# Turning an intermediate by DMA transposes instead of on TensorE, and moving its producer to another PSUM pool

## Chip, cores, metric

One core of a Trainium2 chip. The metric is the device time of one execution in microseconds (us); lower is better. The core's engines are called PE (TensorE matmul), PEld (its weight loads), DVE (VectorE), ACT (ScalarE), POOL (GpSimd) and SP (SyncE, which here only issues DMAs). L394 is line 394 of the kernel that the profile belongs to; the changed file has shifted lines (M4 is L414 before and L418 after, M5 L443 and L447, M2 L376 and L377, scores L253 and L254).

## The reference, cut to what matters

```
attention: 8 batches, 8 heads, 576 positions, head size 64, window of 32 plus 8 global positions
x  = attention output as [batch, 576, 512]
h  = relu(xT @ w_tok1) @ w_tok2            # over the tokens:  M1 (relu), M2
u  = x + hT
out = u + relu(u @ w_ch1) @ w_ch2          # over the channels: M4 (relu), M5
```

M4 multiplies over the channels of u, which M2 leaves with the tokens on the partitions. So u has to be turned first: M3.

## The kernel before

The batches are pipelined. While M5 of batch b runs, M2 and M3 of batch b+1 and the score steps S and GK of batch b+2 are woven between its units; this stage ("the M5 stage of b") is where the change works. PSUM has three pools: `psS` (two buffers of two banks), `psV` (one buffer of two banks) and `psM` (two buffers of one bank, for M4 and M5). PSUM is the memory into which PE writes its results; a buffer goes to the next user only when the engine that reads it (DVE or ACT here) is done. "Exps" are the exponentials of the scores on ACT, "masks" the multiplications of these by the window mask on DVE (four in a row, 2.45 us together), GK the scores against the global positions, and a "unit" of M5 three matmuls. "Start to start" is the time from the start of one group of PE instructions to the start of the next.

```python
def M2(b, part, get):                       # part 0: tokens 0-255, 1: 256-511, 2: the last 64
    ps = get([P, 2, 512])
    ...                                     # 4, 4 or 2 matmuls
    if part < 2: nc.vector.tensor_add(out=s["u16"][...], in0=x16[...], in1=ps)
    else:        nc.vector.tensor_add(out=s["ul"][r], in0=x16[r, NT - 1], in1=ps[r, 0])

def M3(b, part, get):
    if part < 2:
        pu = get([P, 2, 4, P], F16)
        for i in range(2):
            for cc in range(4):
                nc.tensor.transpose(out=pu[:, i, cc, :], in_=s["u16"][:, 2*part + i, P*cc : P*cc + P], identity=ident)
        nc.vector.tensor_copy(out=s["uT"][...], in_=pu)
    else: ...                               # the remainder: odd batches only, for two batches at once

def M4(b, j): ...                           # 4 matmuls, rhs = all 512 tokens of uT; relu on ACT
def S_step(b, hg, part):                    # takes BOTH buffers of psS
    tiles = [pss([P, 2, 512]) for i in range(2)]
    S_mm(...); then exps on ACT             # after parts 1, two units later: four masks on DVE

def phase_m(b):
    u = [(0.9, M2 part 0 in psv), (0.9, M2 part 1 in pss), (0.5, M2 part 2 in pss)]
    u += [(0.5, M3 part 0 in psv), (0.5, M3 part 1 in pss)] + [(0.3, M3 part 2 in psv)]   # the last: odd b

def phase_s(b): return [(0.5, S step) x 4] + [(0.9, GK in psv)]
def mix(m, s): return m[:2] + s[:1] + m[2:3] + s[1:2] + m[3:4] + s[2:3] + m[4:] + s[3:]
# merge(sparse, dense) spreads such a list over the units of M5 (3 matmuls each) by the weights
```

The softmax here doesn't subtract the row's maximum and nothing guards it: scores larger than these inputs give would overflow.

## Time and profile before

| | before |
|---|---|
| device time, median of the three runs known before the prediction | 338.13 us (337.34 to 340.27) |
| profiled span | 336.1 us |
| PE busy | 316.1 us, 94% |
| length of the M5 stages of batches 2 to 6 | 18.85, 20.31, 18.43, 20.31, 13.63 us |

A stage runs from the start of its first M5 matmul to the start of the next M4. Odd stages have 20 units of M5 and even ones 16; the last has no scores beside it. The profile lines behind this table are in the prediction.

### The profile page before, as it was taken

The numbers are of one execution on the slowest core, as the hardware profiler recorded it, in microseconds if no ns is written. First come the engines' busy times: TensorE is split into PE (matmuls) and PEld (weight loads), VectorE is DVE, ScalarE is ACT, GpSimd is POOL, SyncE is SP. The second block draws the span as 40 slices with busy tenths as digits, with TensorE's granted clock in tenths as the row PEclk, the third lists the DMA queues.
The fourth block names the chain that finished last, engine by engine and source line by source line (L and its number), as shares of the span: only waits on it lengthen the run. The fifth ranks groups of instructions, "written<-read, shape, count | busy, mean of one in ns | idle before, by whom it ended". The sixth has DMA issues, their size and how long they took to land.

```text
span 336.1 us, 7493 instructions
## 1 busy us (share of the span) xinstructions
PE 316.1 (94%) x3092; PEld 162.2 (48%) x3092; DVE 193.9 (58%) x361; ACT 158.1 (47%) x295; POOL 75.5 (22%) x154
## 2 busy tenths in 40 slices
PE   7499999988999999999999999999999999999994
PEld 2236443634465445444565446444565446444641
DVE  7698686758566487356762486457573475162021
ACT  5482584125862663528443654438442554403600
POOL 5794160181341032101410033002400000000000
PEclk9789999999999999999999999999999999999999
DMA  7999979999999979503980158001000111011013
GB/s 158 184 246 225 172 135 175 226 181 248 230 194 250 181 221 240 103 34 91 249 179 2 62 170 209 0 34 64 33 2 23 41 68 30 0 64 62 2 62 94
DMA packets 55702, 41.55 MB, mean 124 GB/s; under 512 B 40948, under 2 KB 46964, under 8 KB 55668
## 3 DMA queue, kind: packets, MB, share of 16 engines
q1 hardware_dynamic: 50100, 36.59, 45.4%
q0 software_dynamic: 5568, 4.49, 8.7%
q8 instruction: 24, 0.39, 0.5%
q14 instruction: 10, 0.08, 0.1%
HBM read 36.12 MB, written 9.44 MB: 136 GB/s over the span
## 4 chain that ended last, share of the span: by engine, by line
PE 78%; ACT 7%; DVE 6%; DMA 5%; issue 2%; POOL 1%; SPq 0%; ACTq 0%; DVEq 0%; POOLq 0%
PE op L443 23%; PE b1p L414 22%; PE s L253 5%; PE hp L376 5%; PE a1p L360 4%; DMA q<-in_q_dram 4%; PE b1lp L430 3%; DVE e_all L279 3%; ACT e_all L262 3%; PE w L102 3%; PE pv L335 3%; PE pv L327 2%; PE pv L340 2%; PE gk L294 2%; PE pu L394 2%
## 5 line engine op out<-in xcount | busy, mean ns | idle before, releaser
L414 PE MATMUL b1p<-uT,wc 128*128 128x512 f16 x384 | 92.9, 379 | 1.9 <-DVE b L418 0.8
L443 PE MATMUL op<-wc,b 128*128 128x512 f16 x384 | 94.6, 379 | 0.0
L420 ACT ACTIVATE b<-b1p 128x512 f16<-128x512 f32 x90 | 53.9, 599 | 62.6 <-PE b1p L414 62.3
L443 PEld LDWEIGHTS <-b 128*128 128x128 f16 x384 | 34.8, 97 | 38.8 <-issue 4.2
L414 PEld LDWEIGHTS <-wc 128*128 128x128 f16 x384 | 34.2, 97 | 39.7 <-issue 5.3
L279 DVE TENSOR_TENSOR e_all<-e_all,bandm 128x1000 f16<-128x1000 f16 x64 | 42.0, 717 | 19.1 <-ACT e_all L268 19.0
L262 ACT ACTIVATE e_all<-s 128x800 f16<-128x800 f32 x32 | 25.1, 838 | 38.9 <-PE s L253 38.6
L447 DVE TENSOR_TENSOR osb<-u,op 128x512 f32<-128x512 f16 x32 | 21.9, 686 | 31.5 <-PE op L443 29.4
L381 DVE TENSOR_TENSOR u<-x,hp 128x1024 f16<-128x1024 f16 x14 | 17.1, 1222 | 38.9 <-PE hp L376 38.9
L282 POOL COPY eg<-e_all 128x160 f16<-128x160 f16 x14 | 4.6, 329 | 143.1 <-DVE e_all L279 143.1
L253 PE MATMUL s<-qT,kT 32*128 32x200 f16 (+1 forms) x640 | 22.0, 245 | 7.6 <-DVE qT L202 4.9
L347 DVE TENSOR_TENSOR x<-pv,rr 128x512 f16<-128x512 f32 (+1 forms) x40 | 27.6, 691 | 1.5
L335 PE MATMUL pv<-vsh,e_all 128*128 128x66 f16 x320 | 27.6, 193 | 0.0
L144 POOL CAST k<-k 128x576 f16<-128x576 f32 x28 | 18.7, 698 | 39.5 <-DMA k<-in_k_dram 22.0
L197 POOL CAST vsh<-v 128x512 f16<-128x512 f32 x38 | 24.0, 667 | 11.6 <-DMA v<-in_v_dram 11.6
L335 PEld LDWEIGHTS <-e_all 128*128 128x128 f16 x320 | 24.0, 98 | 4.8
L140 ACT CAST q<-q 128x576 f16<-128x576 f32 x28 | 18.6, 682 | 14.1 <-DMA q<-in_q_dram 7.5
L253 PEld LDWEIGHTS <-kT 32*128 32x128 f16 x640 | 12.6, 95 | 23.4 <-issue 19.3
L340 PE MATMUL pv<-vsh,e_all 128*128 128x66 f16 x256 | 23.4, 193 | 0.0
L102 PE MATMUL w<-zz 128*128 128x512 f16 x66 | 21.9, 448 | 1.3 <-DVE p_i L153 1.3
L376 PE MATMUL hp<-a,w 128*128 128x512 f16 x72 | 19.3, 378 | 2.7 <-ACT a L363 1.6
L327 PE MATMUL pv<-rf,lf 128*128 128x264 f16 x80 | 21.7, 275 | 0.0
(134 smaller groups left out, 354.5 us busy)
## 6 DMA issues: line engine op xcount, KB each, us to landing
q<-in_q_dram SPq DMA_DIRECT2D x64, 128.0 KB
out_dram<-osb SPq DMA_DIRECT2D x32, 256.0 KB
k<-in_k_dram SPq DMA_DIRECT2D x14, 576.0 KB
v<-in_v_dram SPq DMA_DIRECT2D x24, 256.0 KB
v<-in_v_dram SPq DMA_DIRECT2D x16, 192.0 KB
wc<-in_moe_w_ch_dram POOLq DMA_DIRECT2D x6, 512.0 KB, 10.0
q<-in_q_dram SPq DMA_DIRECT2D x16, 64.0 KB
out_dram<-osb SPq DMA_DIRECT2D x8, 128.0 KB
```

Source lines behind the costliest of these rows:

```text
L102: nc.tensor.matmul(ps, lhsT=zz[:, 0:P], rhs=zz, start=True, stop=True)
L253: nc.tensor.matmul(tiles[r // 2][:, r % 2, off : off + n], lhsT=kT[rs, P * c : P * c + P, e], rhs=qf[rs, lo : lo + n, e], start=(e == 0), ...
L262: nc.scalar.activation(out=e2[:, :, 1:3, 64:EW], in_=ps[:, :, 0:400].rearrange("p h (c x) -> p h c x", c=2), func=AF.Exp, scale=scale)
L279: nc.vector.tensor_mul(out=eh, in0=eh, in1=bandm)
L327: nc.tensor.matmul(ps[:, hf, 0 : 4 * VW], lhsT=lfs[b % 2][:, QS * tau - sh : QS * tau - sh + P], rhs=s["rf"][:, 4 * hf : 4 * hf + 4, :], s ...
L335: nc.tensor.matmul(o, lhsT=e_all[:, h, tau, QS - sh : QS - sh + P], rhs=vs[:, tau, h, :], start=False, stop=last and tau == NT - 1,)
L340: nc.tensor.matmul(o, lhsT=e_all[:, h, tau + 1, 0:P], rhs=vs[:, tau + 1, h, :], start=False, stop=last)
L347: nc.vector.tensor_tensor(out=x16[r, tau, :].rearrange("p (f h x) -> p f h x", f=2, h=4), in0=pq[r, :, :, 0:D], in1=rr[r].unsqueeze(3).to_ ...
L376: nc.tensor.matmul(ps[:, i, :], lhsT=w2[:, ch, P * tau - sh : P * tau - sh + P], rhs=s["a1"][:, ch, :], start=(ch == 0), stop=(ch == 1),)
L414: nc.tensor.matmul(ps, lhsT=wc1[:, cc, P * j : P * j + P], rhs=s["uT"][:, cc, :], start=(cc == 0), stop=(cc == 3))
L420: nc.scalar.activation(out=s["b1"][:, j, :], in_=ps, func=AF.Relu)
L443: nc.tensor.matmul(ps, lhsT=w, rhs=wc2[:, j, :], start=(j == 0), stop=(j == NJ - 1))
```

## The change

It takes M3 off PE for batches 3 to 7: u goes from SBUF to SBUF through DMA transposes issued on SyncE. With M3 out of PSUM, all three parts of M2 of these batches draw on `psv`, which leaves `psS` to the scores. And the list for the stage becomes M2, S, M2, S, M2, S, S, GK, with the scores' weights raised from 0.5 to 1.6, which spreads them over the M5 units. The layout of uT changes to make each transpose's output contiguous.

```diff
+TDMA = 3
 def M3(b, part, get):
-            s["uT"] = mb.tile([P, 4, 512], F16, ...)
+            s["uT"] = mb.tile([P, 4, 4, P], F16, ...)
+        if b >= TDMA:
+            if part < 2:
+                nc.sync.dma_start_transpose(out=s["uT"][:, 2*part : 2*part + 2], in_=s["u16"][:, 2*part : 2*part + 2])
+            else:
+                nc.sync.dma_start_transpose(out=s["uTl"], in_=s["ul"])
 def M4(b, j):
-  rhs=s["uT"][:, cc, :]
+  rhs=s["uT"][:, :, cc, :]
 def phase_m(b):
+        if b >= TDMA:
+            u = [(c, lambda i=i: M2(b, i, psv)) for i, (c, _) in enumerate(u)]
+            return [(c, lambda f=f, i=i: (f(), M3(b, i, None)) if i < 2 or b % 2 else f()) for i, (c, f) in enumerate(u)]
 def mix(m, s):
+        if len(m) == 3:
+            s = [(1.6, f) for _, f in s[:4]] + s[4:]
+            return m[:1] + s[:1] + m[1:2] + s[1:2] + m[2:] + s[2:]
```

(Cut: the copies into the new layout for batches 0 to 2.)

More of the change, by code (lines that the diff above doesn't have):

```diff
@@ L388, in M3 @@
         if part == 0:
-            s["uT"] = mb.tile([P, 4, 512], F16, tag="uT", name=f"uT_{b}")
-        if part < 2:
+            s["uT"] = mb.tile([P, 4, 4, P], F16, tag="uT", name=f"uT_{b}")
+        if b >= TDMA:
+            if part < 2:
+                nc.sync.dma_start_transpose(out=s["uT"][:, 2 * part : 2 * part + 2], in_=s["u16"][:, 2 * part : 2 * part + 2])
+            else:
+                s["uTl"] = mb.tile([P, 4, P], F16, tag="uTl", bufs=1, name=f"uTl_{b}")
+                nc.sync.dma_start_transpose(out=s["uTl"], in_=s["ul"])
+        elif part < 2:
             pu = get([P, 2, 4, P], F16, name=f"pu_{b}_{part}")
@@ L396, in M3 @@
                     )
-            nc.vector.tensor_copy(
-                out=s["uT"][:, :, 256 * part : 256 * part + 256].rearrange("p c (i x) -> p c i x", i=2),
-                in_=pu.rearrange("p i c x -> p c i x"),
-            )
+            nc.vector.tensor_copy(out=s["uT"][:, 2 * part : 2 * part + 2], in_=pu)
         else:
@@ L414, in M4 @@
             nc.tensor.matmul(
-                ps, lhsT=wc1[:, cc, P * j : P * j + P], rhs=s["uT"][:, cc, :], start=(cc == 0), stop=(cc == 3)
+                ps, lhsT=wc1[:, cc, P * j : P * j + P], rhs=s["uT"][:, :, cc, :], start=(cc == 0), stop=(cc == 3)
             )
@@ L555, in M3t @@
         if tau == 0:
-            s["uT"] = mb.tile([P, 4, 512], F16, tag="uT", name=f"uT_{b}")
+            s["uT"] = mb.tile([P, 4, 4, P], F16, tag="uT", name=f"uT_{b}")
         pu = get([P, 4, P], F16, name=f"pu0_{b}_{tau}")
@@ L559, in M3t @@
             nc.tensor.transpose(out=pu[:, cc, :], in_=s["u16"][:, tau, P * cc : P * cc + P], identity=ident)
-        nc.scalar.copy(out=s["uT"][:, :, P * tau : P * tau + P], in_=pu)
+        nc.scalar.copy(out=s["uT"][:, tau], in_=pu)
     def X_units(b):
```

## The prediction

> **What bounds the kernel now.** I read the page first, then the stages by windows, then TensorE (PE) in order of time, then the other engines in the same stretch. M1 and M2 are the token products of a batch, M3 turns its u, M4 and M5 are its channel products, S and GK the scores of a later batch, PV the attention output.
>
> ```profile
> PE 316.1 (94%) x3092; PEld 162.2 (48%) x3092; DVE 193.9 (58%) x361; ACT 158.1 (47%) x295; POOL 75.5 (22%) x154
> ...
> PEclk9789999999999999999999999999999999999999
> DMA  7999979999999979503980158001000111011013
> ...
> PE 78%; ACT 7%; DVE 6%; DMA 5%; issue 2%; POOL 1%; SPq 0%; ACTq 0%; DVEq 0%; POOLq 0%
> ```
>
> PE is busy 94% of the span, no other engine above 58%, and the chain that ended last is 78% PE. The DMA row: full up to slice 16 (134 us), nearly empty from slice 25 (210 us) on. So PE time removed from the later batches counts in full, and transfers there find a free path.
>
> The M3 work sits in the stage in which M5 of batch b runs beside M2 and M3 of batch b+1 and the scores of b+2. The windows over this stage for b = 2 to 6 (columns: stretch, length, busy us and count of each engine, granted clock, DMA share, GB/s):
>
> ```profile
> 141.80:160.65 18.85, 18.01 (x191) 8.41 (x190) 11.04 (x17) 10.53 (x22) 1.55 (x3) 1.00 0.24 76
> 180.05:200.36 20.31, 20.08 (x201) 9.30 (x199) 11.92 (x17) 10.62 (x22) 1.56 (x4) 1.00 0.28 90
> 216.94:235.37 18.43, 18.01 (x191) 8.40 (x190) 11.03 (x17) 10.63 (x22) 2.16 (x4) 1.00 0.12 45
> 254.78:275.09 20.31, 20.08 (x202) 9.30 (x200) 11.91 (x17) 8.39 (x18) 0.32 (x1) 1.00 0.15 53
> 291.67:305.30 13.63, 13.63 (x80) 6.79 (x78) 7.01 (x9) 0.60 (x1) 0.00 (x0) 1.00 0.16 59
> ```
>
> The clock is full, DVE and ACT have room, DMA is at 0.12 to 0.28. Inside the third of these, PE in order of time:
>
> ```profile
> 222.55 0.82 PE L443 MATMUL op<-wc,b 128*128 128x512 f16 x3
> 223.53 0.59 PE L376 MATMUL hp<-a,w 128*128 128x512 f16 x2 [0.16 <-ACT e_all L262]
> ...
> 226.54 0.61 PE L394 MATMUL pu<-ident,u 128*128 128x128 f16 x8
> 226.99 0.81 PE L443 MATMUL op<-wc,b 128*128 128x512 f16 x3
> 227.73 0.90 PE L253 MATMUL s<-qT,kT 32*128 32x200 f16 x16
> 228.56 0.82 PE L443 MATMUL op<-wc,b 128*128 128x512 f16 x3
> 229.54 0.61 PE L394 MATMUL pu<-ident,u 128*128 128x128 f16 x8 [0.16 <-ACT e_all L262]
> 229.98 0.81 PE L443 MATMUL op<-wc,b 128*128 128x512 f16 x3
> ```
>
> Two readings. Eight transposes (L394) hold PE from 226.54 to 226.99: 0.45 us, or 56 ns each; the duration of one in its row, 219 ns, overlaps its neighbours and is not the cost. And three M5 matmuls take 0.65 us (229.98 to the next start at 230.63), but after 222.55 the M2 starts only at 223.53: 0.33 us lost, released by the exp of the scores (ACT, L262). Scores take both buffers of their PSUM pool; M2 parts 1 and 2 and M3 part 1 draw from that same pool, so they wait for the exps. That is the wait which the second half of the change attacks.
>
> **What the Trainium skill says.** "Perfetto Trace Analysis", section "Optimization Strategy": the same gap repeating on the saturated engine can mean that PSUM is short for the next tile. The trace agrees: the gap before M2 part 2 returns in all four stages with scores (0.3 to 0.4 us). "VectorE: DVE Perf Modes", section "The three transpose paths": a 128x128 bf16 transpose takes 390 ns on TensorE and 1309 ns by the DMA crossbar. For PE the trace decides, 56 ns of PE time in a stream; it has no DMA transpose. "DMA: Bandwidth & Descriptors": section "Anatomy of one DMA — SWDGE (gpsimd) path" gives a fixed cost of about 2.0 us, and "Latency and other measured facts" an effective 261 GB/s for DMA transposes. On the fixed cost this trace only shows a store on the other kind of queue:
>
> ```profile
> 331.56 0.69 DVE L450 TENSOR_TENSOR osb<-ul,op 128x512 f32<-128x512 f16 x1 [1.90 <-PE op L443]
> 332.28 1.11 SPq L452 DMA_DIRECT2D out_dram<-osb  x2
> ```
>
> SyncE needs 0.55 us to issue each of the two last stores, and the span ends at 336.07, 2.7 us after the second issue: the same order as 2.0.
>
> **The change, part by part.** (1) Removed from PE: batches 3 to 7 lose 16 transposes each, and 3, 5 and 7 the 4 of the shared remainder: 92 in all, 92 x 56 ns = 5.1 us, all in a stage that PE fills. This counts in full. (2) Removed from DVE: 10 copies of 0.69 us and 3 of 0.41 us, 8.1 us. DVE is busy some 11 of 18 to 20 us there, so this is worth nothing directly. (3) PSUM: M2 now draws on the PV pool, which is idle in this stage but for GK at its end. I added up the PE waits tied to the score pool from start-to-start times. Stage b=2: 0.33 before M2 part 2, 0.28 to 0.35 inside the third score step, 0.75 before M3 part 1, 1.4 together. b=4: 0.33 + 0.28 + 0.33 = 0.94. b=3 and 5: 0.39 each. b=6 has no scores and no loss. Sum 3.1 us. The new order spaces the score steps 2 to 4 us apart, and the exps of one need 1.7 us (two of 0.84) or 2.2 us (measured from the end of a part-1 step at 225.9 to the release inside the next at 228.1), so most of it goes. I take 2.6. Single-buffered, M2 part 1 must wait until the add has read part 0; the add ends 1.4 us after part 0 (0.20 us start delay + 1.22 us of L381), and 2.6 us of M5 lie between: no wait. The 0.34 us lost at the start of M4 after the even stages, where an M5 add stands behind the masks on DVE, stays.
>
> (4) Added: per batch two DMA transposes of 256 KB (eight 128x128 blocks each), and one of 128 KB for odd batches, on SyncE. My estimate for one of 256 KB: issue 0.6 to 1.5 us, 256 KB at the skill's 261 GB/s 1.0 us, fixed 2.0 us: 3.6 to 4.5, call it 4.7 with a little delay at the queue. Time to hide it: I worked through the order of the units by their weights, with the durations of this trace (M5 unit 0.65, M2 0.86/0.86/0.43, scores 0.55/0.53, GK 1.19). In stages 2 to 5 M2 part 1 ends at 5.5 to 6.2 us, its add 1.4 later, and M4 of that batch starts at 16 us (even) or 18.5 (odd): 9 to 11 us, hidden. In stage 6 there are no scores to spread it: M2 part 1 comes after nine of sixteen M5 units, ends at 7.55, the add at 8.97, and M4 of batch 7 is due at 12.52. 3.55 us are there for 4.7, so PE stalls some 1.2 us, once. The 128 KB transfer of the remainder is needed only after all of M4 (10 us) and is hidden. (5) The layout of uT changes M4's moving operand to four runs of 128 elements; I expect no change of its 216 ns.
>
> Sum: 338.1 - 5.1 - 2.6 + 1.2 = **331.6 us**, 1.9% less.
>
> **Rivals.** *The transfer becomes the bound.* If the eight blocks of a transfer go one after another at the skill's 1309 ns, one takes 10.5 us and the two of a batch 21. In stage 6 the first starts at 4.2 us, the second ends at 25, M4 stalls 12.7 us; stages 2 to 5 stall some 7 us each; total near 370. Against it: the same page calls this path one with about 90% of the DMA bandwidth, and the order of the units looks placed for a latency of several us. A middle form, 6 to 8 us per transfer, stalls only batch 7, by 2.5 to 4.5 us: 333 to 335. *The gain moves to another wait.* Without the pool wait PE may catch up with the exps, the q casts between them on ACT (0.7 us each), or the M5 adds behind the masks on DVE; then only the transposes are won: 338.1 - 5.1 + 1.2 = 334. For it: at b=2 two casts stood before the exps and cost 0.75 us; against: ACT is at 10.6 of 18 to 20 us. *SyncE in order.* A transpose that waits for u holds the stores and loads behind it. SyncE mostly waits for M5 adds anyway, the loads for batch b+4 stand after the transposes, and three output buffers cover 7.8 us: I expect nothing. *Everything hidden*, with a transfer under 3.5 us and all 3.1 us of waits gone: 338.1 - 8.2 = 329.9.
>
> **Range and chances.** The first sum and the hidden case span 329.9 to 331.6, the lost-gain and middle cases 333 to 335, and the serial case lies far above. I put 8 in 10 on 329.0 to 338.0. The line of 2% is at 331.4, next to my number, so faster by over 2% has 0.46, within 2% 0.44, slower 0.10, which is the serial transfer.
>
> **What would show it.** Right: no L394 or L404 work in stages 2 to 6; these stages shorter by 1.1 to 2.5 us with scores and by 1.1 without; the lines with a wait on L262 gone from M2; M4 of batch 7 starting 1 to 2 us after the last M5 of batch 6, released by the DMA of uT. Wrong: a DMA wait of uT before M4 of batches 3 to 6 (transfer over 9 us), a stall of over 5 us before batch 7, M4 matmuls above 216 ns apart, or the lost time back as waits of the score steps on ACT.

## The result, and the profile after

| | before | after |
|---|---|---|
| median | 337.85 us | 328.60 us (328.19 to 329.14) |
| ratio of the fast runs | | 0.9715 (0.9673 to 0.9757) |
| profiled span | 336.1 us | 327.4 us |

A ratio is the mean time of one kernel's fast runs over that of the other's fast runs of the same rounds, so not quite the ratio of the medians. In a later group of runs the unaltered changed kernel gave 329.04 us against 337.57, ratio 0.9757 (0.9742 to 0.9773). By the two ratios the change is faster by 2.4 to 2.9%; 328.6 lies 0.4 us below the predicted range.

The page after, the lines that answer to those of before:

```profile
PE 308.2 (94%) x3000; PEld 156.3 (48%) x3000; DVE 186.5 (57%) x348; ACT 158.0 (48%) x295; POOL 75.3 (23%) x154
...
DMA  7999969999999969914891559025101320043012
```

92 matmul records are gone, 8 us of PE's busy time (in which durations count, not the time that PE was held), and the DMA row shows new work after slice 20. The windows of the same five stages (columns as in the prediction):

```profile
141.82:158.06 16.24, 16.24 (x171) 7.13 (x170) 9.45 (x14) 10.53 (x22) 0.94 (x2) 1.00 0.42 104
177.46:196.30 18.84, 18.84 (x186) 8.32 (x184) 10.59 (x15) 10.64 (x22) 0.94 (x2) 1.00 0.46 123
212.88:229.12 16.24, 16.24 (x172) 7.14 (x171) 9.45 (x14) 10.53 (x22) 1.55 (x3) 1.00 0.42 90
248.52:267.35 18.83, 18.83 (x185) 8.32 (x182) 10.59 (x15) 8.38 (x18) 0.32 (x1) 1.00 0.30 84
283.93:296.45 12.52, 12.52 (x60) 5.66 (x59) 5.11 (x6) 0.60 (x1) 0.00 (x0) 1.00 0.39 105
```

PE is now busy for the whole of every stage (16.24 of 16.24 us, before 18.01 of 18.85). The stages are shorter by 2.61, 1.47, 2.19, 1.48 and 1.11 us, 8.86 in all, and the span by 8.7: the result lies in these five stages. Of the other stages from M4 of batch 1 on none differs by over 0.02 us but the last, from the first M5 of batch 7 to the end of the last store: 17.87 us against 17.66. Of the 8.86, the removed transposes are 92 x 56 ns = 5.15; the last stage shows it pure, 20 x 56 ns = 1.12 against 1.11 measured. The other 3.71 us are waits that went. PE in order of time in the third of these stages:

```profile
217.55 1.03 PE L377 MATMUL hp<-a,w 128*128 128x512 f16 x4
218.41 1.46 PE L447 MATMUL op<-wc,b 128*128 128x512 f16 x6
219.80 0.60 PE L254 MATMUL s<-qT,kT 32*128 32x136 f16 x24
220.34 1.47 PE L447 MATMUL op<-wc,b 128*128 128x512 f16 x6
221.65 0.59 PE L377 MATMUL hp<-a,w 128*128 128x512 f16 x2
```

The M2 part 2 (the group of two on L377) follows the M5 units with no "idle before" mark; before, it had one, released by the exps. And the start of M4 of batch 7, all engines in order of time:

```profile
291.68 1.22 DVE L382 TENSOR_TENSOR u<-x,hp 128x1024 f16<-128x1024 f16 x1 [0.82 <-PE hp L377]
292.93 1.25 SPq L393 DMA_TRANSPOSE uT<-u  x1
...
296.45 1.03 PE L418 MATMUL b1p<-uT,wc 128*128 128x512 f16 x4
```

The add of M2 part 1 ends at 292.90, the transpose is issued at once, and M4 starts at 296.45, exactly when it is due (stage length 12.52, as worked out): the predicted stall is not there. The same 3.5 us in windows of half a microsecond:

```profile
293.50:294.00 0.50, 0.50 (x4) 0.22 (x3) 0.37 (x1) 0.00 (x0) 0.00 (x0) 1.00 0.00 0
294.00:294.50 0.50, 0.50 (x4) 0.19 (x2) 0.32 (x1) 0.00 (x0) 0.00 (x0) 1.00 0.75 151
295.50:296.00 0.50, 0.50 (x4) 0.19 (x2) 0.50 (x1) 0.00 (x0) 0.00 (x0) 1.00 1.02 381
```

The last two columns are the DMA share and GB/s. Nothing moves in the 1.25 us that SyncE needs to issue; then the DMA engines fill up. By the trace's DMA records the 1024 packets of 256 bytes start between 294.1 and 295.6 (a store of M5 output starts before they end).

### The profile page after: what moved, and what is told of

Same layout as the page of the kernel before. It is cut to its first block, busy times and chain, and to the rows that moved or that the text cites. A ratio compares the mean times of both kernels' runs of the same rounds, so it can differ in the third digit from the quotient of the medians.

```text
span 327.4 us, 7329 instructions
## 1 busy us (share of the span) xinstructions
PE 308.2 (94%) x3000; PEld 156.3 (48%) x3000; DVE 186.5 (57%) x348; ACT 158.0 (48%) x295; POOL 75.3 (23%) x154
## 4 chain that ended last, share of the span: by engine, by line
PE 71%; DMA 14%; DVE 4%; SPq 4%; ACT 3%; POOL 2%; issue 1%; POOLq 0%; DVEq 0%; ACTq 0%
PE op L447 26%; PE b1p L418 21%; DMA q<-in_q_dram 7%; PE hp L377 5%; DMA v<-in_v_dram 4%; PE a1p L361 4%; PE s L254 4%; PE b1lp L434 3%; SPq L95 2%; DMA wc<-in_moe_w_ch_dram 2%; PE pv L336 2%; DVE e_all L280 2%; PE pv L328 2%; PE pv L341 2%; PE gk L295 1%
## 5 line engine op out<-in xcount | busy, mean ns | idle before, releaser
L447 PE MATMUL op<-wc,b 128*128 128x512 f16 x384 | 92.5, 379 | 0.0
L263 ACT ACTIVATE e_all<-s 128x800 f16<-128x800 f32 x32 | 25.2, 841 | 29.1 <-PE s L254 28.9
L254 PE MATMUL s<-qT,kT 32*128 32x200 f16 (+1 forms) x640 | 20.8, 244 | 6.9 <-DVE qT L203 4.4
L254 PEld LDWEIGHTS <-kT 32*128 32x128 f16 x640 | 11.9, 95 | 22.2 <-issue 18.3
L377 PE MATMUL hp<-a,w 128*128 128x512 f16 x72 | 19.3, 379 | 1.9 <-ACT a L364 1.5
```

Source lines behind the costliest of these rows:

```text
L254: nc.tensor.matmul(tiles[r // 2][:, r % 2, off : off + n], lhsT=kT[rs, P * c : P * c + P, e], rhs=qf[rs, lo : lo + n, e], start=(e == 0), ...
L263: nc.scalar.activation(out=e2[:, :, 1:3, 64:EW], in_=ps[:, :, 0:400].rearrange("p h (c x) -> p h c x", c=2), func=AF.Exp, scale=scale)
L377: nc.tensor.matmul(ps[:, i, :], lhsT=w2[:, ch, P * tau - sh : P * tau - sh + P], rhs=s["a1"][:, ch, :], start=(ch == 0), stop=(ch == 1),)
L447: nc.tensor.matmul(ps, lhsT=w, rhs=wc2[:, j, :], start=(j == 0), stop=(j == NJ - 1))
```

## The experiments

The table gathers the stage lengths from the profiles, which are steadier than whole times: the M5 stage of batch 0, long before the stages that differ, took between 21.5 and 24.4 us from one profile to the next, of this kernel and of others. That alone moves whole times by up to 3 us, and the stages below do not show it. Most of it goes with the granted clock: the four profiles with 24.3 to 24.4 us there (`e2_dma_old_pool`, `e3_layout_only`, `e4_late13`, `e7_pe_new_order`) show a clock of 0.5 for 3.4 us from about 73 us on, the ten with 21.5 to 22.5 us do not.

| M5 stage of batch | 2 | 3 | 4 | 5 | 6 | sum |
|---|---|---|---|---|---|---|
| before | 18.85 | 20.31 | 18.43 | 20.31 | 13.63 | 91.5 |
| pools alone | 19.17 | 19.77 | 19.17 | 19.83 | 13.93 | 91.9 |
| change, M2 parts 1 and 2 in the score pool | 18.52 | 20.01 | 18.52 | 20.07 | 12.52 | 89.6 |
| change, only M2 part 1 in the score pool | 16.32 | 18.83 | 16.31 | 18.83 | 12.52 | 82.8 |
| change, old score weights | 17.33 | 19.20 | 17.34 | 19.20 | 12.52 | 85.6 |
| PE transposes, spread order, PV pool | 20.86 | 20.01 | 21.95 | 20.01 | 13.93 | 96.8 |
| change | 16.25 | 18.83 | 16.24 | 18.83 | 12.52 | 82.7 |

**Layout alone** (`e3_layout_only`), a control.

```diff
-TDMA = 3
+TDMA = 8
```

> The changed file with no batch switched over: only the new layout of uT and the plain copies into it remain. Theory A, the layout costs and wins nothing: within 0.2 us of the kernel before, M4 matmuls 216 ns apart, the copies 0.69 us. Rival B, part of the unpredicted gain of 2 to 3 us comes from the layout (cheaper copies, better reads): 0.5 us or more faster than before.

Measured: 337.37 us against 337.34, ratio 0.9997 (0.9973 to 1.0021); copies 688 ns and M4 matmuls 216 ns apart in both. The layout is worth nothing.

**Pools alone** (`e1_pool_only`): transposes on PE in the old order, M2 and M3 all in `psv`.

```diff
-u = [(0.9, M2 part 0 psv), (0.9, M2 part 1 pss), (0.5, M2 part 2 pss)]; M3: psv, pss, psv
+u = all parts of M2 in psv for b >= 3;                                  M3: psv, psv, psv
```

> The kernel before with one part of the change: TensorE transposes and the old order of units stay, but from the fourth batch on M2 and M3 draw only on the PV pool, so that the scores have theirs alone (the new layout of uT is in, too). Theory A, the 3.1 us of PE waits in the four stages with scores come from sharing the score pool: most of them go, 2.0 to 2.8 us, so 335 to 335.8 us against 337.7, ratio 0.992 to 0.994. Rival B, the waits move on to the score steps themselves, which in the old order follow each other too closely for the exps: under 1 us, ratio above 0.997.

Measured: 337.64 us against 337.34, ratio 1.0022 (1.0001 to 1.0044): nothing won, theory A fell. The waits are still there under other names. All engines in the stage of batch 4:

```profile
226.62 2.45 DVE L280 TENSOR_TENSOR e_all<-e_all,bandm 128x1000 f16<-128x1000 f16 x4 [0.96 <-ACT e_all L269]
...
228.98 0.68 DVE L404 COPY uT<-pu 128x1024 f16<-128x1024 f16 x1
...
229.72 0.61 PE L401 MATMUL pu<-ident,u 128*128 128x128 f16 x8 [0.82 <-DVE uT L404]
```

The first M3 part had left PE at 226.5, but its copy stands behind four masks on DVE and ends at 229.66; the one buffer of `psv` is taken until then, and the second M3 part waits 0.98 us (from start-to-start times). Not quite my rival B either: the wait went to M3's own copies, and the third score step kept the 0.36 us that it had before. By stages the table shows more than the total: the pool alone took 0.54 and 0.48 us off the two odd stages with their 20 units, and cost 0.32, 0.74 and 0.30 us in the even ones. (This run moves M3 part 1 into `psv` as well, which the change doesn't need; M2 moved alone was not run.)

**The change with M2 parts 1 and 2 back in the score pool** (`e2_dma_old_pool`).

```diff
-u = [(c, lambda i=i: M2(b, i, psv)) for ...]
+u = [(c, lambda i=i: M2(b, i, pss if i else psv)) for ...]
```

> The changed kernel with one part undone: M2 parts 1 and 2 draw on the score pool again; DMA transposes and the new order of units stay. Theory A, with the scores spread out and M3 gone from PE the sharing costs little: by the order of the units 0.3 to 0.5 us in each even stage and 0 to 0.2 in each odd one, together 0.6 to 1.4 us, so 329.2 to 330.0 against 328.6. Rival B, the PSUM part of the change is what removed the waits: they come back, 0.4 to 1.4 us per stage as before, 3 us in all, near 331.7.

Measured: 336.25 us, ratio to the kernel before 0.9964 (0.9941 to 0.9987). Both theories were far off: of the change's 8.9 us in the stages 7.0 are lost again, more than all the waits of the kernel before. Where, in the stage of batch 4:

```profile
227.52 0.59 PE L377 MATMUL hp<-a,w 128*128 128x512 f16 x2
227.68 2.44 DVE L280 TENSOR_TENSOR e_all<-e_all,bandm 128x1000 f16<-128x1000 f16 x4
...
230.15 0.69 DVE L385 TENSOR_TENSOR ul<-x,hp 64x512 f16<-64x512 f16 x1
...
230.89 0.53 PE L254 MATMUL s<-qT,kT 32*128 32x200 f16 x14 [1.94 <-DVE ul L385]
```

M2 part 2 ends at 228.1, its add runs only at 230.15, after four masks, and the next score step needs that buffer: 2.19 us lost.

**Only M2 part 1 in the score pool** (`e9_part1_old_pool`, one look), formed on that reading.

```diff
+u = [(c, lambda i=i: M2(b, i, pss if i == 1 else psv)) for ...]
```

> The changed kernel with only M2 part 1 back on the score pool (the run with parts 1 and 2 there lost 2.28 us in each even stage and 1.2 in each odd one). Theory A, those losses come from part 2: its PSUM buffer is free only when its add is done, the add stands behind four masks on DVE, and the next score step needs the buffer. Part 1 has no mask before its add, so here the even stages stay at 16.2 to 16.4 us and the odd ones at 18.8 to 19.0. Rival B, any M2 part in the score pool makes a score step wait: even stages 1 us or more longer.

Measured: even stages 16.32 and 16.31 us, odd ones 18.83, as theory A said. So it is not sharing as such that costs, but a buffer whose release stands behind the masks in DVE's order.

**The old score weights** (`e6_old_spacing`).

```diff
-s = [(1.6, f) for _, f in s[:4]] + s[4:]
+s = [(0.5, f) for _, f in s[:4]] + s[4:]
```

> The changed kernel with one number undone: the score steps get their old weight 0.5 instead of 1.6, so the last two steps follow each other after one M5 unit in even stages. Theory A, the spacing is a third part of the change that matters: the fourth score step waits for the exps of the third, about 1.1 us in each even stage and 0.4 in each odd one, 2.5 to 3.5 us in all, and the masks at the end come later still; near 332. Rival B, DMA transposes and the PV pool alone do it: within 0.7 us of the changed kernel.

Measured: 330.48 us, ratio 0.9807 (0.9762 to 0.9851); stages longer by 1.09 and 0.37 us, 2.9 in all, of which the M4 stages after the even ones give 0.5 back. Theory A's wait is there. Its later masks did not cost M4 anything, and the whole time stays below its "near 332". PE in the stage of batch 4, the fourth score step:

```profile
225.23 0.24 PE L254 MATMUL s<-qT,kT 32*128 32x136 f16 x2 [0.30 <-ACT e_all L263]
225.96 0.60 PE L254 MATMUL s<-qT,kT 32*128 32x136 f16 x22 [0.49 <-ACT e_all L263]
```

It waits for each of the two exps of the third (L263).

**PE transposes in the spread order** (`e7_pe_new_order`): everything but the DMA.

```diff
-b >= TDMA: M3 by DMA
+b >= TDMA: M3 on PE, PSUM from psv; order M2, S, M2, S, M3, S, M2, M3, S, (M3,) GK with weight 1.6
```

> TensorE transposes, all of M2 and M3 on the PV pool, score steps spread with weight 1.6 as in the change. Theory A, the PV pool has one buffer, and without DMA transposes it also waits for the copies of uT, which stand behind the masks on DVE: 1.5 us or more of waits per even stage, total no better than 2 us below the kernel before, 335.5 to 338. Rival B, the DMA transposes are worth just their 5.1 us of PE time and the rest is order and pools: then this one has all of that rest, 3.7 us, near 334.

Measured: 343.0 us, ratio 1.0171 (1.0122 to 1.0219), slower than before, and worse than theory A's range. In the stage of batch 4 the line that costs most is

```profile
239.67 1.68 PE L295 MATMUL gk<-qT,kg 32*32 32x512 f16 x32 [2.50 <-DVE uTl L410]
```

GK waits for a copy of the remainder's uT, which again stands behind four masks: 2.65 us, start to start. (Of the 21.95 us of this stage, 1.1 more than that of batch 2, another part goes with a granted clock of 0.5 for 3.4 us from 240.3 us on.) So in this arrangement, with one buffer in `psv`, the order and the pool pay only once M3 needs no PSUM.

**How long a transfer takes** (`e4_late13` and `e4_late11`, one look each): in the stage of batch 6, the second M2 part of batch 7 after 13 or 11 of the 16 M5 units instead of 9.

```diff
+if b == 6: D5[:3] + M2 part 0 + D5[3:n] + M2 part 1 + D5[n:14] + M2 part 2 + D5[14:]     # n = 13, 11
```

> The changed kernel, but in the stage of batch 6 the second M2 part of batch 7 is moved from after 9 to after 13 of the 16 M5 units: its add then ends 0.95 us before M4 of batch 7 is due instead of 3.55. The stall in front of M4 is then the time from the end of the add to the data of the transpose being usable, less 0.95. Theory A, from the trace of the changed kernel: issue on SyncE 1.25 us, packets 1.45 us, completion 0.5 to 0.8: 3.2 to 3.5 us, so a stall of 2.2 to 2.6. Rival B, the prediction's estimate of 4.7 us: a stall of 3.75 (the changed kernel, which shows none with 3.55 us to spare, already speaks against it). Rival C, the transpose is usable soon after its last packet: under 2.0.

> As the run with the second M2 part of batch 7 after 13 units (stage of batch 6 14.88 us long instead of 12.52, a stall of 2.36 with 0.95 us to spare, so 3.31 us from the end of the add to usable data), but after 11 units: 2.25 us to spare. Theory A, the 3.31 us are a fixed latency of one transfer: stall 3.31 - 2.25 = 1.06 us, stage 13.6 us. Rival B, the stall of the other run came from something else that moved with the M2 part (its own add, the remainder's transfer in the queue): the stall is then not 1.3 us shorter.

Measured: stage 14.88 us with n = 13 and 13.48 with n = 11, so 2.36 and 0.96 us more than 12.52. The chain that ended last, with n = 13:

```profile
296.30 1.23 DVE u L382
297.53 0.02 issue
297.54 3.24 DMA uT<-u
300.79 0.05 issue
300.83 2.38 PE b1p L418 x10
```

From the end of the add to M4 are 3.30 us, from the issue on SyncE 3.24. (Of the 2.36 us, 0.83 were already lost before M2 part 2, which here waited for the add of part 1 in the one buffer of `psv`; the chain gives the latency without that.) With n = 11 it is 3.21 us from the add's end (293.01) to M4 (296.22); there the view names an M5 add as releaser, which can't be it, as M4 of the changed kernel starts ahead of that add. The two agree, and theory A of both holds: in this quiet stage a latency of 3.2 to 3.3 us, of which issue is 1.25 and packets some 1.5.

**Going further.** `e5_tdma2` sets TDMA = 2, `e8_best_t3` the weights to 1.4 for scores and 2.0 for GK, `e8_best_t2` both; `a0_after` is the changed kernel beside the last two.

> The changed kernel with batch 2 switched over as well (from the third batch on). Theory A, the gain of an odd stage comes again: that stage (M5 of batch 1) goes from 20.3 to 18.8 us, total 1.5 us below the changed kernel, ratio to the kernel before near 0.967. Rival B, the DMA queue is full there (DMA row 0.7 to 0.9 at 104 to 125 us): the transposes wait behind loads on SyncE and in the queue, M4 of batch 2 stalls by 2 us or more, and nothing or less than nothing is won.

> The weights alone (1.4 and 2.0), batch 2 not switched over. Theory A: the even stages as long as in the changed kernel (16.24 us), the first M4 after them 0.26 us shorter (19.14 in place of 19.40), so 0.5 us in all: not to be told from the changed kernel by its time, only by its stages. Rival B, even stages longer by 0.3 us or more.

> The changed kernel with batch 2 switched over too and the score weights at 1.4 (scores) and 2.0 (GK), which puts the last score step and its masks one M5 unit earlier. Theory A: 1.1 us from the stage of batch 1 (as the run with batch 2 switched over showed), and the 0.34 us lost at the start of M4 after each of the two even stages gone, because the M5 add no longer stands behind the masks: 1.5 to 1.8 us below the changed kernel, ratio near 0.968. Rival B, the earlier last step runs into the exps of the third and gives the 0.3 us back in the same stage: then only the 1.1 us.

> The changed kernel once more, unaltered, as the measure for the other runs of this group: ratio 0.971 to 0.974 to the kernel before.

| | median us | ratio to before |
|---|---|---|
| `e5_tdma2` | 327.68 | 0.9722 (0.9662 to 0.9783) |
| `a0_after` | 329.04 | 0.9757 (0.9742 to 0.9773) |
| `e8_best_t3` | 329.54 | 0.9760 (0.9723 to 0.9797) |
| `e8_best_t2` | 328.60 (five fast runs; a sixth, 333.15, is slow) | 0.9738 (0.9713 to 0.9764) |

None can be told from the changed kernel by its time (328.60 and 329.04 in its two groups; `e5_tdma2` had no run of it beside it). The ratios of `a0_after` and `e8_best_t2` missed what was expected (0.971 to 0.974, near 0.968); that of `e5_tdma2` was near 0.967 only within its wide interval. By stages, the weights do what was expected: the M4 stages after even ones 19.14 us instead of 19.40. TDMA = 2 took 1.09 us off the M5 stage of batch 1 in one profile, of a fast run (19.22 against 20.31; 1.5 was expected). The missing 0.4 us is a wait of M4. Loads stand before the transposes on SyncE there, so the second was issued at 116.95 though its u was ready at 111.04, and it then took 5.66 us to be usable, where the quiet stage had 3.24:

```profile
116.95 5.66 DMA uT<-u
122.61 0.05 issue
```

In the profile of `e8_best_t2`, which counts as slow (333.15 us), the same stage took 21.27 us, and M4 came later still:

```profile
116.86 2.91 SPq L393 DMA_TRANSPOSE uT<-u  x1
119.87 2.46 SPq L452 DMA_DIRECT2D out_dram<-osb  x1
122.43 1.30 SPq L393 DMA_TRANSPOSE uT<-u  x1
...
125.77 1.04 PE L418 MATMUL b1p<-uT,wc 128*128 128x512 f16 x2 [2.28 <-DMA uT<-u]
```

The first transpose and a store take SyncE 2.9 and 2.5 us to issue where they need 1.3 and 0.4 in the quiet stages, at a DMA share of 1.1 (2.0 and 0.5 in the fast profile at the same share), and the second transpose starts late; its own latency is 3.3 us here. The M4 stage after it took 20.70 us against 17.35, beside a low granted clock (the third column from the end):

```profile
125.70:132.60 6.90, 5.46 (x12) 1.54 (x12) 2.73 (x5) 1.19 (x2) 3.89 (x10) 0.51 1.01 251
```

This is one slow profile, and how often that happens was not measured, so I would keep TDMA = 3.

## Why the prediction was wrong

The direction and the place were right, the size was not: 6.5 us were predicted, 9.25 measured by the medians (8.5 in the later group) and 8.7 by the profiles. Two terms of the sum failed: the stall of step (4), 1.2 us predicted and none found, and the waits of step (3), 2.6 us predicted and 3.7 gone.

- *Step (1), transposes on PE, 5.1 us in full*: right. The stage without scores lost 1.11 us for 20 of them.
- *Step (4), a stall of 1.2 us before batch 7*: the term that was mis-sized most. The margin of 3.55 us was right (stage 12.52 as worked out); the transfer takes 3.3 us, not 4.7, so it fits with 0.25 us to spare. I had allowed for the issue within 0.6 to 1.5 us (it is 1.25), but a whole 2.0 us of fixed cost came on top of issue and movement, where 0.5 to 0.6 was left (1.8 with the issue, so the 2.0 would have covered both). Then came a further 0.2 to 1.1 of margin for the queue, with no row behind it.
- *Step (3), PSUM waits, 2.6 us*: 3.71 went. 0.5 of the difference is a discount for which no line stood; 0.55 are waits inside the score steps that my sum left out, start to start against the same step after: 0.08 in the first step of each even stage, 0.2 in the fourth of each odd one. The text also calls the PV pool idle but for GK; in the kernel before, M2 part 0 and one or two parts of M3 draw on it too.
- Together: 331.6 - 1.2 - 1.1 = 329.3, and with the median of before at 337.85 instead of 338.1, 329.0. The rest to 328.6 is within what the stage of batch 0 varies by.
- *The parts add up*: this is the step that failed in kind, though it did not show in the total. I gave pool and order together 2.6 us of their own, beside the 5.1 of the transposes. In the stages, pool and spread order without the DMA lose 5.2 us (`e7_pe_new_order`; 1.1 of them beside the low clock), the pool alone loses 0.3 (`e1_pool_only`), and all the rest without M2's new pool wins 1.9 (`e2_dma_old_pool`), less than the 5.15 of the transposes, so that 3.3 us of waits were added; together they win 8.9. In the even stages the pool helps only after M3 has left PSUM. What the spread order or the DMA transposes would give with the old pools and otherwise nothing changed, no run shows.
- *Step (2), DVE's 8.1 us of copies are worth nothing directly*: true for its busy time, and it hid the point. The copies and adds that free a PSUM buffer stand in DVE's order behind 2.45 us of masks. That, more than the exps on ACT that the waits of before name, decides what a PSUM buffer costs in the variants that lost most (`e1_pool_only` in its even stages, `e2_dma_old_pool`, `e7_pe_new_order`); `e6_old_spacing` lost to the exps themselves.
- *Step (5), layout*: right (ratio 0.9997). The 0.34 us at the start of M4 after the even stages stayed, as said (these M4 stages take 19.40 us after the change and 19.41 before).
- *Rivals*: the serial transfer at 1.31 us per block is out, as 256 KB take 3.3 us. "The gain moves to another wait" did not happen in the change, but is just what happens when it is done by halves. SyncE's order did no harm from batch 3 on; with batch 2 switched over it did, by 0.4 us in the fast profile and more in the slow one.

## What to carry to other kernels

Before giving a PSUM buffer to a product, ask what will free it and what stands before that instruction on its engine: here a short add behind four masks cost 2.2 us in each even stage, which the engine's busy share doesn't tell. The DMA transpose was a good trade here, where PE was the bound, DMA was quiet and the consumer at least 3.5 us away, because it removes a PSUM buffer and a copy as well as PE time. And parts of a change that release the same resource need not add up: price the combinations, or test each alone, before giving each a share.

## What the Trainium skill lacked or had wrong

- "VectorE: DVE Perf Modes", section "The three transpose paths", gives 1309 ns for one 128x128 block by the DMA crossbar and no time for several in one transfer. Here one DMA transpose of eight blocks (256 KB) took 3.24 us from issue to use in a quiet stage, so 0.4 us per block, not eight times 1.31; in a busy one a transpose took 5.66 us.
- The same section's 390 ns for TensorE is not what a transpose costs in a stream, and the section doesn't say so: one held PE for 56 ns here (a duration of 219 ns in its row).
- "DMA: Bandwidth & Descriptors", section "Latency and other measured facts", gives 261 GB/s for DMA transposes with a non-contiguous middle dimension, and more for the contiguous case. Here 256 KB moved as 1024 packets of 256 bytes in about 1.45 us, some 180 GB/s, partly beside a store. Its fixed cost of about 2.0 us ("Anatomy of one DMA — SWDGE (gpsimd) path") is for the other kind of queue; here about 0.55 us were left after issue and packets, or 1.8 us with the issue.
- No time was found there for what a DMA transpose costs the issuing engine on this chip (a section on a later chip has counts of cycles for earlier ones): 1.25 us of SyncE for 256 KB and 1.19 for 128 KB on a quiet queue, and at a DMA share of 1.1 up to 2.0 us in a fast run and 2.9 in a slow one.
